# Loading x in halves of 64 partitions on two queues, in a Trainium2 kernel that sums a gated long convolution and a gated MLP

## The chip, the cores and the metric

The kernel runs on one core of a Trainium2 chip. The metric is the device time of one execution in microseconds (us), of which three runs of the kernel before are known: 233.98, 233.99 and 234.03, median 233.99. One execution was also taken by the profiler; its trace covers 232.4 us from the first instruction to the last.

## The reference

```python
x  = A_q                                   # (1, 2048, 640) bf16
xn = layernorm(x)                          # over the 640 features, no gain or bias
# branch A: a short convolution of k over 4 taps, times v, then a convolution over all
# 2048 positions with ssm_k (by FFT of length 4096), a skip term, and a gate by xn
kv = shift_conv(A_k, A_shift_k) * A_v
a  = xn * (irfft(rfft(kv) * rfft(A_ssm_k))[:2048] + kv * A_ssm_D)
# branch B: a gated MLP, 640 -> 1728 -> 640
b  = (sigmoid(xn @ B_w_gate) * (xn @ B_w_up)) @ B_w_down
out = x + a + b
```

## The kernel before, in words

The 2048 rows of x are laid out as 128 partitions by 16 blocks: row 16p + b stands on partition p in block b, so one block is 128 rows of 640 bf16 values, 1280 bytes each and 160 KB together, with its rows 20 KB apart in DRAM. Tile `x` holds all blocks; it receives the results too (`down_ev`, L320, and `inv2_x`, L498, add into it) and is stored to `out` from there (`store`, L323).

The MLP runs in four groups `t` of four blocks (512 rows). Group 0 has to be normalised before any product can start, and this is the opening that the change touches:

1. L501 to L505 load the blocks 0 to 3. Blocks 0 and 1 load as two column halves each, columns 0 to 319 on SP's queue (`sync`) and columns 320 to 639 on ACT's queue (`nc.scalar`). Block 2 is one transfer on SP, block 3 one on ACT. Each queue so issues 80, 80 and 160 KB.
2. L506 to L508 put the first four weight loads (320 KB each) behind them on SP: gate and up columns 0 to 255, then gate and up columns 256 to 511.
3. For each block VectorE (DVE) takes the statistics of the two column halves (`ln_stats`, L198), joins them (L202) and adds epsilon (L210); GpSimd (POOL) takes the power -0.5 (L214); DVE writes the normalised block (`ln_xn`, L219). TensorE (PE) turns it in five transposes (`xn_mm`, L244), and ScalarE (ACT) copies the turned block out of PSUM (`xn_ev`, L247).
4. PE meanwhile runs 10 products on zeros (`busy`, L515), and 3 more after block 0's transposes. Then come the quarter products (`quarter`, L262), a block of 128 rows at a time for the first two feature tiles of gate and up, each needing one turned block. From the third feature tile on, whole products of 512 rows run (`product`, L271).

After that, every step of the kernel comes from a string of letters written out by hand (`ORDER`), each letter the next step of one chain: "g" the MLP's products, "m" the early loads, "o" the stores, and so on. The tail of the order is the last `down_mm` steps, with the last block's columns 512 to 639 as the very last product, then `down_ev` on DVE, then the store of those 128 columns (L662): 128 rows of 256 bytes, 32 KB, on SP.

The compiled program gives each DMA one of eight completion semaphores in turn. A DMA whose semaphore was used before waits, on the engine that issues it, until the earlier DMA with that semaphore has landed. Before, six x loads and the first two weight loads take the eight semaphores, and the third weight load is the first that waits.

Of the kernel before, what the change touches and what calls it, by code (L numbers as in the profile page):

```python
# [17 lines left out]
DM = 640  # L18
FF = 1728
P = 128  # L20
NB = S // P
# [36 lines left out]
def kernel(  # L58
# [14 lines left out]
    nc = tc.nc  # L73
    xr = A_q.flatten_outer_dims().rearrange("(p b) d -> p b d", b=NB)
    kr = A_k.flatten_outer_dims().rearrange("(p b) d -> p b d", b=NB)
    vr = A_v.flatten_outer_dims().rearrange("(p b) d -> p b d", b=NB)
    outr = out.flatten_outer_dims().rearrange("(p b) d -> p b d", b=NB)
# [27 lines left out]
    x = res.tile([P, NB, DM], BF16, name="x")  # L105
# [15 lines left out]
    sync = nc.sync  # L121
# [201 lines left out]
        sync.dma_start(outr[:, b0:b1, lo:hi], x[:, b0:b1, lo:hi])  # L323


    def add_D(c):
        h0 = cin[c]["kvh"][0:1, 1, 0:2, :].rearrange("p b c -> p (b c)").rearrange("p (c e) -> p e c", e=2)[:, 0, :]
        nc.gpsimd.tensor_tensor(h0, h0, cin[c]["dr"][:, :], ALU.add)
# [169 lines left out]
        nc.vector.tensor_tensor(xs, xs, chunks[c]["yx", m][:, :, :], ALU.add)  # L498


    for b in range(2):  # L501
        for i in range(2):
            (sync, nc.scalar)[i].dma_start(x[:, b, 320 * i:320 * i + 320], xr[:, b, 320 * i:320 * i + 320])
    for i in range(2):
        (sync, nc.scalar)[i].dma_start(x[:, 2 + i, :], xr[:, 2 + i, :])  # L505
    for lo in (0, 256):  # L506
        for u in range(2):
            load_w(sync, lo, lo + 256, u)  # L508
# [43 lines left out]
    def step(k, fn, *args):  # L552
        chains[k].append((fn, args))
# [48 lines left out]
    for c in range(NC):  # L602
        for n in range(2):
            step("H", h_turn, c, n)
        step("D", add_D, c)
        for n in range(8):
            step("a", st1_mm, c, n)
# [51 lines left out]
    for b in range(12, NB - 1):  # L659
        step("o", store, b, b + 1, 0, DM)  # L660
    step("o", store, NB - 1, NB, 0, 4 * P)
    step("o", store, NB - 1, NB, 4 * P, DM)  # L662

    ORDER = """
    mmggmmsgmuggmsgmgsuZumgggssumkgkguskugkkmsgugmmmmgkgmksgmuggHskkHkgsmukkgDumsgggkusumgTmkgkukagaumHg
# [44 lines left out]
```

## Time and profile before

| what | value |
|---|---|
| median of three runs | 233.99 us (233.98 to 234.03) |
| profiled execution: span | 232.4 us |
| PE busy | 227.3 us, 98% of the span |
| DVE busy | 203.9 us, 88% |
| ACT busy | 123.0 us, 53% |
| SP's DMA queue (q1) | 90.6% of 16 engines' span |
| ACT's DMA queue (q10) | 0.5% |
| first DMA issue / first statistics on DVE | 0.72 us / 3.02 us |
| last instruction of DVE ends | 229.89 us |

The profile records the span of its execution only; the runs' time is 1.6 us longer than the span. Busy time of PE is modelled for pipelined matmuls, so that neighbouring rows overlap. A DMA row is the issue on the engine that issues it ("SPq", "ACTq"); the transfer itself runs later, and the profile gives for some of them the time from issue to landing. All times in a view are from the span's start.

### The profile page before, as it was taken

How to read it: one execution, taken by the hardware profiler on the slowest of the kernel's cores; microseconds unless marked ns; L12 is line 12 of the kernel's file. 1: busy time of each engine (PE TensorE's matmuls, PEld its weight loads, DVE VectorE, ACT ScalarE, POOL GpSimd, SP SyncE). 2: the span in 40 equal slices, each digit the busy share in tenths (PEclk: the TensorE clock that was granted, in tenths of full speed). 3: DMA queues.
4: the chain of work that ended last, by engine and by line, in shares of the span. 5: the costliest groups of instructions: out<-in, count | busy, mean ns of one | idle time of the engine just before them, and what ended most of it. 6: DMA issues, size and time to landing. Idle time of an engine off the chain costs nothing.

```text
span 232.4 us, 5436 instructions
## 1 busy us (share of the span) xinstructions
PE 227.3 (98%) x2201; PEld 130.7 (56%) x2201; DVE 203.9 (88%) x362; ACT 123.0 (53%) x154; POOL 13.3 (6%) x26
## 2 busy tenths in 40 slices
PE   7999999999999999999999999999999999999995
PEld 2754445877454556667554544478654544446772
DVE  5534799999989999999999999997799999997773
ACT  2433232595354877766775847673555667752000
POOL 5210010040001100000010300000000000000000
PEclk9999999999999999999999999999999999999999
DMA  6999999799999979999989999597989998364784
GB/s 179 320 328 238 265 312 293 201 249 148 336 209 322 290 263 241 273 210 237 331 236 268 272 258 300 171 218 203 260 247 276 290 257 246 119 170 115 224 265 136
DMA packets 96303, 56.79 MB, mean 244 GB/s; under 512 B 55894, under 2 KB 90518, under 8 KB 96022
## 3 DMA queue, kind: packets, MB, share of 16 engines
q1 hardware_dynamic: 95846, 56.12, 90.6%
q8 instruction: 17, 0.28, 0.5%
q10 hardware_dynamic: 432, 0.33, 0.5%
q14 instruction: 8, 0.07, 0.1%
HBM read 36.12 MB, written 18.35 MB: 234 GB/s over the span
## 4 chain that ended last, share of the span: by engine, by line
PE 95%; DVE 2%; DMA 1%; ACT 0%; issue 0%
PE pd L315 27%; PE pu L271 24%; PE pg L271 24%; PE psb L488 4%; PE ps L376 4%; PE ps L374 4%; PE ps L418 3%; PE psa L447 2%; PE pg L292 2%; DVE st L198 1%; DMA x<-in_A_q_dram 1%; PE pu L262 1%; PE pg L262 1%; PE pt L244 0%; DVE xn L219 0%; ACT xnT L247 0%
## 5 line engine op out<-in xcount | busy, mean ns | idle before, releaser
L271 PEld LDWEIGHTS <-w 128*128 128x128 bf16 x500 | 46.6, 98 | 54.2 <-issue 4.7
L315 PE MATMUL pd<-wd,hT 128*128 128x320 bf16 (+2 forms) x448 | 66.0, 299 | 0.0
L271 PE MATMUL pg<-xnT,w 128*128 128x512 bf16 x250 | 62.2, 379 | 0.1
L271 PE MATMUL pu<-xnT,w 128*128 128x512 bf16 x250 | 62.2, 379 | 0.0
L315 PEld LDWEIGHTS <-hT 128*128 128x128 bf16 x448 | 41.7, 98 | 18.2 <-issue 2.4
L280 ACT ACTIVATE sig<-pg 128x512 bf16<-128x512 f32 x52 | 31.1, 601 | 31.1 <-PE pg L271 27.3
L286 DVE TENSOR_TENSOR hT<-sig,pu 128x512 bf16<-128x512 bf16 x52 | 34.9, 680 | 11.6 <-PE pu L271 7.5
L234 ACT CAST xz<-ps 128x1024 bf16<-128x1024 f32 x36 | 35.1, 1014 | 15.8 <-PE ps L418 15.7
L234 ACT CAST t<-ps 128x1024 bf16<-128x1024 f32 x24 | 23.7, 1013 | 16.3 <-PE ps L376 14.1
L433 DVE TENSOR_TENSOR xz<-xz 128x2048 bf16<-128x2048 bf16 x20 | 24.4, 1219 | 0.2
L376 PE MATMUL ps<-kvh,S1t 128*128 128x128 bf16 x160 | 21.4, 219 | 0.0
L374 PE MATMUL ps<-kvh,S1t 128*128 128x128 bf16 x160 | 21.4, 217 | 0.0
L354 DVE TENSOR_TENSOR acc<-acc,tmp 128x1024 bf16<-128x1024 bf16 x30 | 20.4, 681 | 0.3
L352 DVE TENSOR_TENSOR tmp<-kx,sc 128x1024 bf16<-128x1024 bf16 x30 | 20.4, 680 | 0.3
L320 DVE TENSOR_TENSOR x<-pd,x 128x320 bf16<-128x320 f32 (+2 forms) x32 | 15.2, 482 | 3.8 <-PE pd L315 3.6
L374 PEld LDWEIGHTS <-S1t 128*128 128x128 bf16 x160 | 15.5, 97 | 2.5
L376 PEld LDWEIGHTS <-S1t 128*128 128x128 bf16 x160 | 15.4, 96 | 2.5
L234 ACT CAST TBt<-ps 128x1024 bf16<-128x1024 f32 x14 | 13.8, 1012 | 4.0 <-PE ps L376 3.9
L198 DVE BATCH_NORM_STATS2 st<-x 128x6 f32<-128x320 bf16 x32 | 13.9, 475 | 1.9 <-DMA x<-in_A_q_dram 1.9
L493 DVE TENSOR_TENSOR yx<-psb,xn 128x512 bf16<-128x512 f32 x20 | 13.7, 686 | 1.4 <-PE psb L488 0.8
L431 DVE STREAM_SHUFFLE xz<-xz 128x512 f32<-128x512 f32 x20 | 14.6, 728 | 0.0
L234 ACT CAST ao<-psa 128x1024 bf16<-128x1024 f32 x9 | 9.0, 1013 | 8.3 <-PE psa L447 6.9
(55 smaller groups left out, 159.8 us busy)
## 6 DMA issues: line engine op xcount, KB each, us to landing
t<-d SPq DMA_DIRECT2D x15, 512.0 KB, 6.0
d<-t SPq DMA_DIRECT2D x13, 512.0 KB, 4.9
d<-TBt SPq DMA_DIRECT2D x7, 512.0 KB, 5.8
d<-ao SPq DMA_DIRECT2D x6, 512.0 KB, 5.5
bi<-d SPq DMA_DIRECT2D x6, 512.0 KB, 5.3
kx<-in_A_k_dram SPq DMA_DIRECT2D x10, 256.0 KB, 5.9
hn<-in_A_ssm_k_dram SPq DMA_DIRECT2D x20, 128.0 KB, 5.0
kvh<-in_A_v_dram SPq DMA_DIRECT2D x10, 256.0 KB, 5.2
```

What stands on the lines that cost most here:

```text
L198: nc.vector.bn_stats(d["st"][:, i, s2, :], x[:, b, s2 * 320:(s2 + 1) * 320])
L234: nc.scalar.copy(out=out, in_=in_)
L271: nc.tensor.matmul(pg[:, :], lhsT=w[:, c, u * UP + fc * P:u * UP + (fc + 1) * P], rhs=xnT[:, :, c, :], start=(c == 0), stop=(c == NC - 1))
L280: nc.scalar.activation(sig[fc][:, :], pgs[0, fc][:, :], ACT.Sigmoid)
L286: nc.vector.tensor_tensor(hT[:, fc, :], sig[fc][:, :], pgs[1, fc][:, :], ALU.mult)
L315: nc.tensor.matmul(pd[:, :], lhsT=hT[:, fc, bb * P:(bb + 1) * P], rhs=wd[:, fc, es], start=(fc == 0), stop=(fc == NFC - 1))
L320: nc.vector.tensor_tensor(x[:, 4 * t + bb, es], pds[bb, half][:, :], x[:, 4 * t + bb, es], ALU.add)
L352: nc.vector.tensor_tensor(d["tmp"][:, :, :], kx[:, lo + 3 - m:hi + 3 - m, :], sb(m), ALU.mult)
L354: nc.vector.tensor_tensor(d["acc"][:, :, :], d["acc"][:, :, :], d["tmp"][:, :, :], ALU.add)
L374: nc.tensor.matmul(ps[:, i, 0:P], lhsT=S1[:, b, h, :], rhs=cin[c]["kvh"][:, 0, b, :], start=True, stop=True)
L376: nc.tensor.matmul(ps[:, i, P:2 * P], lhsT=S1[:, b, h, :], rhs=hp[:, b // 2, b % 2, :], start=True, stop=True)
L433: nc.vector.tensor_tensor(z[:, 1:3, :, :], z[:, 0:1, :, :].to_broadcast((P, 2, 8, P)), z[:, 1:3, :, :], ALU.mult)
```

## The change

Blocks 0 to 3 load in the same way, each as two transfers of 64 partitions with the full row of 640 values: partitions 0 to 63 on SP, partitions 64 to 127 on ACT. There are eight x loads of 80 KB instead of four of 80 KB and two of 160 KB, four on each queue instead of three. The store of the last 128 columns is split in the same way, 64 partitions on SP and 64 on ACT; the step stays the last one of the chain "o".

```diff
+    def last_store():
+        for i, eng in enumerate((sync, nc.scalar)):
+            eng.dma_start(outr[rows[i], NB - 1, 4 * P:DM], x[rows[i], NB - 1, 4 * P:DM])
+
...
-    for b in range(2):
+    rows = (slice(0, 64), slice(64, P))
+    for b in range(4):
         for i in range(2):
-            (sync, nc.scalar)[i].dma_start(x[:, b, 320 * i:320 * i + 320], xr[:, b, 320 * i:320 * i + 320])
-    for i in range(2):
-        (sync, nc.scalar)[i].dma_start(x[:, 2 + i, :], xr[:, 2 + i, :])
+            (sync, nc.scalar)[i].dma_start(x[rows[i], b, :], xr[rows[i], b, :])
...
-    step("o", store, NB - 1, NB, 4 * P, DM)
+    step("o", last_store)
```

## The prediction

> **What bounds the kernel now.** I read the page's shares first, then who kept PE waiting, then the chain of waits in the first 14 us, then the order of time at both ends.
>
> ```profile
> PE 227.3 (98%) x2201; PEld 130.7 (56%) x2201; DVE 203.9 (88%) x362; ACT 123.0 (53%) x154; POOL 13.3 (6%) x26
> PE 95%; DVE 2%; DMA 1%; ACT 0%; issue 0%
> ```
>
> PE carries 95% of the chain that ended last. The list of PE's waits (us in total, times, longest) has only three entries, all in the opening:
>
> ```profile
> PE idle L515 <- DVE hT L117: 1.2, 1, 1.2
> PE pt L244 <- DVE xn L219: 0.7, 2, 0.4
> PE pg L262 <- ACT xnT L247: 0.2, 1, 0.2
> ```
>
> So once the quarter products run, PE never stops until its last product. The end is the moment at which PE gets going, plus a fixed amount of PE work, plus the tail after the last product. The change touches the first and the last of these. The chain of waits shows what sets the first:
>
> ```profile
> 0.72 2.27 DMA x<-in_A_q_dram
> 2.99 0.02 issue
> 3.02 0.90 DVE st L198 x2
> ...
> 7.04 0.47 PE pt L244 x5
> 7.51 0.02 issue
> 7.53 0.70 ACT xnT L247
> 8.23 0.04 issue
> 8.27 0.72 PE pg L262 x10
> ```
>
> Only one transfer is in it: block 0's, issued at 0.72 and landed at 2.99. Then DVE works without a gap to block 1's normalised rows, PE and ACT turn them, and from 8.27 PE is continuous. Blocks 1 to 3 are not in it: DVE reaches their statistics at 4.25, 5.76 and 7.21, and the semaphore records of the trace have them landed by 3.60, 5.36 and 5.59. A microsecond won or lost at 3.02 is therefore a microsecond of the whole; an earlier landing of block 2 or 3 is worth nothing.
>
> **The opening: the wait that DVE starts on.** Today DVE's first statistics need only the left column half, from SP. The right half, from ACT, landed at 3.18 by the semaphore records, 0.19 later though issued at the same moment, and DVE needs it only after 0.46 us of its own work. With halves by partition, the first statistics span all 128 partitions and wait for both. So the first step of the sum is a loss: with transfers as they are now, DVE starts 0.19 later.
>
> Against this stands a faster transfer. Windows over the opening show what the 16 DMA engines do (last columns: granted clock, DMA share, GB/s):
>
> ```profile
> 1.70:2.20 0.50, 0.50 (x3) 0.17 (x2) 0.00 (x0) 0.50 (x1) 0.50 (x2) 1.00 0.48 122
> 2.20:2.70 0.50, 0.50 (x3) 0.15 (x1) 0.00 (x0) 0.45 (x2) 0.50 (x2) 1.00 1.11 322
> 3.00:3.20 0.20, 0.20 (x2) 0.00 (x1) 0.18 (x1) 0.00 (x0) 0.03 (x1) 1.00 2.27 179
> 3.20:3.70 0.50, 0.50 (x2) 0.15 (x1) 0.50 (x2) 0.00 (x0) 0.00 (x0) 1.00 0.36 65
> ```
>
> Two things in it. First, packet cost: between 2.20 and 2.60 the two queues used 60.5% and 55.5% of 16 engines for 234 packets, 1.16 x 16 x 400 / 234 = 32 ns each, nearly all of 640 bytes. The 1280-byte stores at 228.5 to 230.1 used 86.7% for 430 packets, 46 of them tiny: about 57 ns for one of 1280 bytes. Block 0 is 256 packets of 640 now and 128 of 1280 then: 16 x 32 = 512 ns an engine against 8 x 57 = 456, 0.06 us less. Second, supply: in the first half microsecond of packets the engines are busy 0.48 of the time, because packets arrive one by one. If packets arrive at the same rate but carry twice the bytes, that idle time, 0.5 x 0.52 = 0.26 us, could shrink to nothing; it could also stay, if it comes from how fast each engine's queue is opened. So block 0's second half lands between 3.18 - 0.06 - 0.26 = 2.86 and 3.18. I take the packet term whole and a quarter of the supply term, 3.18 - 0.06 - 0.06 = 3.06, since the later queue opens when the engines are already filling (322 GB/s from 2.20 on). Against 2.99 that is **+0.07 us**, bounds -0.13 and +0.19.
>
> The Trainium skill has a rule that speaks against this edit (page "DMA: Bandwidth & Descriptors", section "Rules for kernel authors"): two transfers to disjoint partition halves serialise, since both spray over all 16 engines, and one transfer of 128 partitions is to be used. The trace agrees that both queues share the engines (60.5% and 55.5% in one window); by the rule the supply term would be nothing, and the opening +0.13.
>
> **What else moves in the opening.** The issues: SP issues four x loads instead of three, at 0.40 to 0.45 us each, so the first gate weights go out at about 2.55 to 2.6 instead of 2.12. This costs nothing: their data waits behind the x data anyway (they landed at 6.63, and PE first wants them at 7.33, 0.70 later). The cover is that 0.70. The semaphores: eight x loads fill the eight, but the first gate load takes one that ACT has not yet reached, so ACT's last x load (block 3, partitions 64 to 127) waits for block 0's landing, and the first up weights wait for block 0 as well. ACT's load goes out at about 3.1 instead of 1.65. Behind it on ACT stands the copy of the turned block 0 at 6.08, 3 us away. The load needs, by ACT's slower issue-to-landing times (2.5 us by the semaphore records for block 0, 3.9 for block 3), until 5.6 to 7.0; DVE wants it at 7.21. Hidden, by 0.2 us in the worst of the two. The up weights go out at 3.1 instead of 2.59; they landed at 7.75 and PE wants them at 9.11, cover 1.36. All later weight loads wait for the DMA eight places before them, as they do now. Orders on PE, DVE and POOL are the same line for line.
>
> **The tail.** DVE's last addition ends at 229.89. SP issues the last store at 229.97; it lands 1.5 us later, at 231.475, and the program's closing waits run to 232.4.
>
> ```profile
> 228.57 1.77 SPq L323 DMA_DIRECT2D out_dram<-x  x3
> 228.82 1.07 DVE L320 TENSOR_TENSOR x<-pd,x 128x512 bf16<-128x512 f32 x2 [1.15 <-PE pd L315]
> out_dram<-x SPq DMA_DIRECT2D x1, 32.0 KB, 1.5
> ```
>
> Its 128 packets of 256 bytes ran from 230.85 to 231.12, right behind the store before it, which itself landed at 231.25. Halving them saves at most 0.22 us (the store before then ends the program). But now the end waits for an ACT issue as well. ACT is free (its last work ends at 211.9), so nothing is queued behind it, but no row shows ACT issuing a store or anything late. The nearest rows are the opening's: ACT's transfer landed 0.19 (block 0) and 0.2 (3.9 against 3.7 us for blocks 3 and 2) later than SP's twin. Its first packet came 1.26 us after the issue, against 0.88 for the last store on SP: 0.38 is the upper bound. I take 0.2, less 0.07 for four packets fewer an engine at 18 ns: **+0.13 us**, bounds -0.22 and +0.38.
>
> **The sum.** +0.07 + 0.13 = +0.20 on a span of 232.4. The runs' median lies 1.6 us above the span; what lies outside the span does not change, so I add to the median: 234.2 us, +0.09%. A measurement of this kernel tells about 0.2%, 0.47 us, from no change, and the sum is inside that. The bounds together are -0.35 and +0.57: 233.6 to 234.6.
>
> **The rivals.**
>
> *Slower: the stall catches block 0.* In the windows above, DMA throughput collapses from 3.00 to 3.70 (179 and 65 GB/s at up to 2.27 times full share: packets in flight for 0.3 to 1 us). These slow packets are the first 1280-byte ones of blocks 2 and 3; no 640-byte packet took over 0.24. If the stall belongs to that size or row pattern and not to the moment, block 0 meets it. Price, by the rate lost against 331 GB/s: 0.2 x 0.46 + 0.5 x 0.80 = 0.49 us, so +0.69 and 234.7. It decides as soon as 0.27 of the 0.49 falls before block 0's landing. Against it: packets of other sizes are slow too, in bursts all over the trace, and 1280-byte stores late are not. Chance 0.20.
>
> *Slower: ACT's queue is late at both ends.* +0.19 and +0.38 together give +0.57, 234.6. For it: every ACT transfer in the trace is later than its SP twin. Against: smaller transfers should not be as late as larger ones. Chance 0.07.
>
> *Faster: the supply term whole and short issues.* If 64 rows are generated in half the time, block 0 lands at 2.86, and a shorter issue (0.26 us for a one-row load against 0.40) takes 0.14 more; with the tail at its floor, -0.13 - 0.14 - 0.22 = -0.49, 233.5. It needs everything at its best end. Chance 0.13.
>
> *Block 3's ACT half late.* If it queues behind the up weights (landed 7.75) DVE waits 0.5 us at 7.21. The fourth normalised block is done at 9.85 and PE takes it at 10.22, so 0.37 is covered: +0.13 more, 234.3, still no change. Chance 0.05. That the halves are not what runs is excluded by the program: 64x640 loads on both queues.
>
> **How the numbers follow.** The forecast holds 0.55. Within 0.2%: forecast and late block 3, 0.60. Slower: 0.20 + 0.07 = 0.27. Faster 0.13. The range reaches from the edge of the faster case, 233.55, to a little over the stall's price, 234.8; about 0.08 is left out below and as much above. The forecast alone would be 233.7 to 234.45.
>
> **What would show it.** After: DVE's first statistics start at 3.05 to 3.15 with both halves of block 0 landed by then; the statistics stay gapless; PE's quarter products run on from about 8.35; the ACT store lands after the SP one, at about 231.7. A start of DVE before 2.9 says that the supply term was whole; one after 3.4 that a stall came in. A PE wait later than 8.5, or one on weights, would make the reasoning wrong, not only its sizes.

## The result, and the profile after

The changed kernel takes 235.91 us (median of six runs, 235.32 to 237.35). The kernel before took 234.07 (six runs, 233.98 to 234.36). The ratio is 1.0083, 95% interval 1.0056 to 1.0111: slower by 0.8%, and outside the predicted range of 233.55 to 234.8. Two things happened: even the fastest run is 1.34 us above the fastest of before, and the runs of the changed kernel spread over 2 us.

The profiled execution took 235.32, the fastest of the six; its span is 233.5, against 232.4 before. The page:

```profile
PE 227.9 (98%) x2201; PEld 130.9 (56%) x2201; DVE 204.1 (87%) x362; ACT 123.1 (53%) x154; POOL 13.3 (6%) x26
PE 75%; SPq 11%; DVE 6%; DMA 6%; issue 1%; DVEq 0%
```

PE's work is unchanged, but the chain that ended last no longer runs through PE alone: 11% of it is SP issuing DMAs, which had no share before, and 6% is DMA (1% before). The list of PE's waits has a fourth entry, in the middle of the kernel:

```profile
PE idle L518 <- DVE hT L117: 1.2, 1, 1.2
PE pt L244 <- DVE xn L219: 0.7, 2, 0.4
PE pg L262 <- ACT xnT L247: 0.2, 1, 0.2
PE ps L378 <- DVE kvh L361: 0.2, 1, 0.2
```

The opening in order of time (start, duration, engine, line):

```profile
0.72 0.56 ACTq L508 DMA_DIRECT2D x<-in_A_q_dram  x1
0.72 2.77 SPq L508 DMA_DIRECT2D x<-in_A_q_dram  x4
1.37 1.19 ACTq L508 DMA_DIRECT2D x<-in_A_q_dram  x2
3.10 0.47 ACTq L508 DMA_DIRECT2D x<-in_A_q_dram  x1
3.46 0.49 DVE L198 BATCH_NORM_STATS2 st<-x 128x6 f32<-128x320 bf16 x1 [2.34 <-DMA x<-in_A_q_dram]
3.54 0.59 SPq L173 DMA_DIRECT2D w<-in_B_w_gate_dram  x1
```

Each x issue keeps its queue for 0.47 to 0.81 us, where those of before took 0.40 to 0.45. Four of them occupy SP for 2.77 us, so the first weight load goes out at 3.54 instead of 2.12, 1.42 later. DVE starts at 3.46 instead of 3.02, 0.44 later. By the semaphore records ACT's half of block 0 landed first, at 3.08, and SP's at 3.36; the half that DVE needed first before had landed at 2.99. So 0.37 of the 0.44 is the landing. The other 0.07 is a second wait: in all the kernels that were profiled, DVE starts 0.10 after the landing where it waits for two loads, and 0.02 to 0.03 after it where it waits for one. The windows that the prediction used now read:

```profile
1.70:2.20 0.50, 0.50 (x3) 0.18 (x2) 0.00 (x0) 0.50 (x1) 0.50 (x2) 1.00 0.19 28
2.20:2.70 0.50, 0.50 (x3) 0.15 (x1) 0.00 (x0) 0.49 (x2) 0.50 (x2) 1.00 0.86 264
3.00:3.20 0.20, 0.20 (x2) 0.01 (x1) 0.00 (x0) 0.00 (x0) 0.03 (x1) 1.00 1.01 199
3.20:3.70 0.50, 0.50 (x2) 0.15 (x1) 0.24 (x1) 0.00 (x0) 0.00 (x0) 1.00 1.02 264
```

From 1.70 to 2.20 the engines move 28 GB/s, not 122, because the first packet comes at 2.07 instead of 1.76 (ACT's; SP's first comes at 2.44). The supply of packets did not get better but worse. The collapse at 3.2 to 3.7 (65 GB/s before) is gone, so the stall that the prediction feared is not the cause.

The tail:

```profile
229.41 1.07 DVE L320 TENSOR_TENSOR x<-pd,x 128x512 bf16<-128x512 f32 x2 [1.15 <-PE pd L315]
230.52 0.53 ACTq L328 DMA_DIRECT2D out_dram<-x  x1
230.56 0.54 SPq L328 DMA_DIRECT2D out_dram<-x  x1
```

The two stores leave at the moment that one would, but each issue takes 0.53 or 0.54 instead of 0.375. By the semaphore records ACT's half lands at 232.27 and SP's, issued 0.05 after it, at 232.55. From DVE's last end (230.49) to the last landing are 2.07 us; it was 1.58.

The profiled span so divides: PE gets going 0.46 later (whole products from 13.21 instead of 12.75); PE and DVE lose 0.13 on the way to the last addition; the last landing comes 0.49 later after it; the closing instructions take 0.10 more. Together 1.18.

### The profile page after: what moved, and what is told of

It is laid out like the page before. It is cut to its first block, busy times and chain, and to the rows that moved or that the text cites. A ratio compares the mean times of both kernels' runs of the same rounds, so it can differ in the third digit from the quotient of the medians.

```text
span 233.5 us, 5444 instructions
## 1 busy us (share of the span) xinstructions
PE 227.9 (98%) x2201; PEld 130.9 (56%) x2201; DVE 204.1 (87%) x362; ACT 123.1 (53%) x154; POOL 13.3 (6%) x26
## 4 chain that ended last, share of the span: by engine, by line
PE 75%; SPq 11%; DVE 6%; DMA 6%; issue 1%; DVEq 0%
PE pd L315 21%; PE pu L271 18%; PE pg L271 18%; PE psb L492 4%; PE ps L378 3%; PE ps L380 3%; PE ps L422 3%; DMA x<-in_A_q_dram 3%; DMA kvh<-in_A_v_dram 3%; PE psa L451 2%; SPq L173 2%; SPq L176 2%; SPq L139 2%; PE pg L292 1%; DVE st L198 1%
```

## The experiments

The first theory was read off the rows above: **an issue of 64 partitions is dear in itself**, and it costs in three places, DVE's start, SP's stream of loads behind it, and the tail. The rivals: that it is dear only when both queues issue halves together, that it comes from splitting and waiting for two queues, or that only DVE's start and the tail count.

### What an issue costs, by itself

The loop of the first measuring kernel, without the definitions above it (the comment is added here):

```python
for f in 2 * (sp_full, sp_lo, sp_hi, sp_cols, sp_lo_cols, sp_32, sp_96, sp_64x2, act_full, act_lo,
              pair_cols, pair_rows, pair_full):
    nc.vector.memset(y[:, 0:2, :], 0.0)   # holds the next load until this one has landed
    f()
```

> This kernel computes nothing of the reference: it issues single loads of x rows by themselves, each after the one before has landed and DVE has cleared the tile, twice over: on SP 128, 64 (partitions 0 to 63), 64 (64 to 127), 32 and 96 partitions of 640 values, 128 and 64 partitions of 320, 64 partitions of two rows of 320; on ACT 128 and 64 of 640; then pairs on both queues. Theory 'an issue of 64 partitions is dear in itself': every load of 64 partitions keeps its queue 0.15 to 0.25 us longer (about 0.6 us) than one of 128 partitions (about 0.4), alone as well as in pairs, whatever its bytes. Rival 'only together': alone 64 and 128 partitions both take 0.35 to 0.45, and 0.6 only in the pair of partition halves. Rival 'packet size': 64 of 640 takes 0.6, 64 of 320 and 64 of two rows take 0.4.

The kernel ran once. Rows of its timeline, in this order: SP's loads of 64 partitions (0 to 63), 64 (64 to 127), 128 x 320, 64 x 320, 32, 96, two rows of 320 on 64 partitions, and, in the second pass, 128:

```profile
11.26 0.53 SPq L92 DMA_DIRECT2D y<-in_A_q_dram  x1
14.52 0.47 SPq L92 DMA_DIRECT2D y<-in_A_q_dram  x1
17.55 0.33 SPq L92 DMA_DIRECT2D y<-in_A_q_dram  x1
20.34 0.47 SPq L92 DMA_DIRECT2D y<-in_A_q_dram  x1
23.20 0.35 SPq L92 DMA_DIRECT2D y<-in_A_q_dram  x1
25.87 0.32 SPq L92 DMA_DIRECT2D y<-in_A_q_dram  x1
28.71 0.64 SPq L101 DMA_DIRECT2D y<-in_A_q_dram  x1
48.75 0.33 SPq L92 DMA_DIRECT2D y<-in_A_q_dram  x1
```

All the forms with 64 partitions take 0.47 or more, alone on an otherwise idle core; all the others on SP take 0.32 to 0.35, those of 32 and 96 partitions too. So both rivals fail: a load of 64 is dear alone, and with 640 bytes per packet as with 1280 (two rows per partition make it dearer still, 0.64). The difference, 0.14, is a little under the 0.15 to 0.25 that was expected; in the kernel, where one issue follows another, both forms take longer, about 0.42 and 0.60. The packet records add what the issue rows hide: the first packet starts 0.97 us after the issue for 128 partitions and 1.27 for 64, so 0.30 is lost before any data moves. A whole 128-partition block landed after 2.14 us and a 64-partition half, with half the bytes, after 2.15 to 2.38.

The pairs show how block 0 loads in the two kernels. Column halves: SP's landed 2.09 and 2.17 us after the issue (two passes), ACT's 2.27 and 2.34. Partition halves: 2.34 and 2.44, and 2.60 and 2.68. DVE needs SP's column half in the one kernel, the later of both partition halves in the other: 2.09 against 2.60, 0.51 later. The kernel shows 0.44. In the pair ACT's first packet comes 0.17 and 0.19 after SP's for columns, and 0.26 and 0.32 after it for partition halves. This second delay is not special to 64 partitions: with a whole block on each queue it is 0.32 and 0.30. Nor is it always ACT that is later: in the changed kernel SP's first packet came 0.37 after ACT's.

### Which row counts, and the store

The second measuring kernel has the same loop over other forms.

> Like the first measuring kernel (nothing of the reference is computed): single loads of 640 values on SP with 128, 16, 48, 56, 63, 64 (from partition 32), 65, 72, 80 and 112 rows; of two rows of 320 on 32, 96 and 128 partitions; then 96 rows on SP with 32 on ACT; then stores of 128 columns to DRAM: 128 partitions on SP, on ACT, 64 on SP, 64 + 64, 96 + 32, and 64 + 64 columns. 'Exactly 64 rows is dear': only the load from partition 32 takes about 0.47, the others 0.33; 'a range of row counts': some of 48 to 80 take 0.47 too. Stores: 64 on SP takes 0.15 longer to issue than 128; the pair of 64 + 64 lands 0.3 to 0.5 later than the whole store on SP, the pair 96 + 32 within 0.2 of it.

It ran once, too. Loads of 63, 64 (from partition 32), 65 and 72 rows, then the store of 128 partitions on SP and that of 64:

```profile
19.70 0.27 SPq L92 DMA_DIRECT2D y<-in_A_q_dram  x1
22.46 0.61 SPq L92 DMA_DIRECT2D y<-in_A_q_dram  x1
25.62 0.31 SPq L92 DMA_DIRECT2D y<-in_A_q_dram  x1
28.39 0.30 SPq L92 DMA_DIRECT2D y<-in_A_q_dram  x1
52.24 0.37 SPq L97 DMA_DIRECT2D out_dram<-y  x1
56.96 0.51 SPq L97 DMA_DIRECT2D out_dram<-y  x1
```

Of the counts that were tried (16, 48, 56, 63, 64, 65, 72, 80, 112, 128, and 32 and 96 in the first kernel) 64 alone is dear. Landing times of the stores, from the semaphore records, two passes each: whole on SP 1.48 and 1.45 us after the issue, whole on ACT 1.49 and 1.51, 64 partitions on SP alone 1.75 and 1.71, the later one of 64 + 64 1.97 and 1.96, of 96 + 32 1.59 and 1.62, of column halves 1.64 and 1.58. So 64 + 64 costs 0.49 to 0.51 over the whole store, which is the 0.49 of the kernel's tail, and no split of this store wins anything. About half of it is the form alone (1.71 to 1.75 against 1.45 to 1.48), the other half the second place in a pair. The pair of loads of 96 and 32 rows landed 2.30 and 2.28 us after the issue on SP, 2.47 and 2.43 on ACT, also later than SP's column half (2.09 and 2.17). Why 64 is special no run shows.

### The opening alone, the tail alone

The changed kernel with the last store of before:

```diff
-    step("o", last_store)
+    step("o", store, NB - 1, NB, 4 * P, DM)
```

> The opening of the changed kernel with the last store of the kernel before. If the two places add up as in the profiles (PE starts 0.46 us later, about 0.1 us of a wait in the middle, tail 0.5), this one is 0.5 to 0.9 us slower than before in its best runs, with the same spread upwards of 1 to 2 us, since the spread comes from loads that the opening delays; if the spread came from the tail, this one is steady within 0.3 us.

Measured: 235.58 median, lowest 234.56, highest 237.26, where before's 25 runs on that chip had 234.29, 233.86 and 235.86. Ratio 1.0041, interval 1.0010 to 1.0073. Lowest run +0.70, median +1.29, and the spread is there without the split store.

The changed kernel with the opening of before:

```diff
-    for b in range(4):
+    for b in range(2):
         for i in range(2):
-            (sync, nc.scalar)[i].dma_start(x[rows[i], b, :], xr[rows[i], b, :])
+            (sync, nc.scalar)[i].dma_start(x[:, b, 320 * i:320 * i + 320], xr[:, b, 320 * i:320 * i + 320])
+    for i in range(2):
+        (sync, nc.scalar)[i].dma_start(x[:, 2 + i, :], xr[:, 2 + i, :])
```

> The opening of the kernel before with the last store split over both queues. Theory 'longer issue and a late second landing': the end moves by 0.4 to 0.6 us after DVE's last addition, the time by as much (234.4 to 234.7), steady from run to run. By the forecast's own tail term it would be +0.13 (234.2).

Measured: 234.76, lowest 234.41: +0.47 and +0.55; ratio 1.0025, interval 1.0000 to 1.0050. In its profile the last landing is 2.08 us after DVE's last end. The size is as expected; "steady" is a miss, since its runs reach 236.25. But those of before reach 235.86 on the same chip, so the split store need not be the reason. The two halves of the change add up about: 0.70 + 0.55 = 1.25 in the lowest runs against 1.34, and 1.29 + 0.47 = 1.76 in the medians against 1.84.

### SP's stream late, DVE's start not

Against the kernel before:

```diff
+    nc.gpsimd.memset(w[:, 0, 0:1], 0.0)
+    nc.gpsimd.memset(w[:, 0, UP:UP + 1], 0.0)
     for lo in (0, 256):
         for u in range(2):
             load_w(sync, lo, lo + 256, u)
```

> The kernel before, with x loaded as before, but the first weight loads on SP held back until GpSimd has cleared one column of the weight tile (about 3.2 us instead of 2.12): SP's stream is late by about 1.1 us and DVE's start is not. Theory 'the late stream costs by itself': waits appear in the middle (DVE for x's second group of blocks, PE behind it) and the time is 0.3 to 1.5 us longer with a spread. Rival 'only DVE's start and the tail count': the time stays within 0.2 us of before.

Measured: 235.69, lowest 234.62: +1.40 and +0.76; ratio 1.0058, interval 1.0031 to 1.0085. Its profile is of the slowest of its ten runs, 237.27. In it DVE starts at 2.95, and the first weight load goes out at 3.11. The waits of PE and, from 9 to 60 us, of DVE:

```profile
PE ps L374 <- DVE kvh L357: 1.4, 1, 1.4
...
PE ps L374 <- DMA S1t<-tabS: 0.9, 1, 0.9
...
PE ps L374 <- ACT t L234: 0.5, 1, 0.5
```

```profile
DVE kvh L334 <- DMA hn<-in_A_ssm_k_dram: 2.4, 2, 2.1
DVE acc L348 <- DMA kx<-in_A_k_dram: 1.6, 1, 1.6
...
DVE st L198 <- DMA x<-in_A_q_dram: 0.5, 1, 0.5
```

Nothing at PE's start (whole products from 12.79), nothing in the tail (1.58 us): a microsecond on SP's stream comes out again between 22 and 58 us, as waits on later loads of SP, most of them for the convolution. The rival "only DVE's start and the tail count" is refuted by the lowest run as well as by the median; the size of these waits is that of the slowest run. The changed kernel's own profile has the same waits, small, since it is the fastest run:

```profile
DVE st L198 <- DMA x<-in_A_q_dram: 0.3, 1, 0.3
DVE acc L352 <- DMA kx<-in_A_k_dram: 0.2, 1, 0.2
```

### The same split at 96 and 32

Against the changed kernel, at both places:

```diff
-    rows = (slice(0, 64), slice(64, P))
+    rows = (slice(0, 96), slice(96, P))
```

> The changed kernel with 96 and 32 partitions instead of 64 and 64, at both places: same number of transfers, queues, semaphores and waits. 'The dear issue of 64 rows is the cause': DVE starts at 3.0 to 3.15, SP's first weight load goes out at about 2.6, the tail is within 0.2 us of before; time 234.2 to 234.6, the blind forecast's world. Rival 'splitting by partition and waiting for both queues costs, whatever the row count': as the changed kernel, 235.3 to 237.

Measured: 234.62, lowest 234.37, against 234.20 and 233.98 for before: +0.42 and +0.39; ratio 1.0022, interval 1.0006 to 1.0038. The opening:

```profile
0.72 1.81 SPq L508 DMA_DIRECT2D x<-in_A_q_dram  x4
2.57 0.43 SPq L173 DMA_DIRECT2D w<-in_B_w_gate_dram  x1
3.27 0.89 DVE L198 BATCH_NORM_STATS2 st<-x 128x6 f32<-128x320 bf16 x2 [2.16 <-DMA x<-in_A_q_dram]
```

Number of transfers, queues, semaphores and waits are those of the changed kernel. With issues of 0.40 to 0.43 on SP the first weights leave at 2.57, not 3.54, and the tail takes 1.68 us instead of 2.07. So the dear form of 64 rows makes most of the change: 1.34 in the lowest runs shrinks to 0.39. What is left is the cost of the split as such, by this profile 0.25 at DVE's start (3.27 against 3.02) and 0.10 in the tail. The start was expected at 3.0 to 3.15 and is later: SP's 96 rows landed at 3.17, and the second wait adds its 0.07. This profile is of the slowest of its twelve runs (236.07). It shows a wait in the middle: 1.5 us of PE behind DVE's L361, itself behind `hn` and x loads.

### Two versions with fewer issues on SP

The kernel before with whole blocks (only the new lines are shown):

```diff
+    for b in range(4):
+        (sync, nc.scalar)[b % 2].dma_start(x[:, b, :], xr[:, b, :])
```

> The kernel before with blocks 0 to 3 as whole 128-partition transfers, 0 and 2 on SP, 1 and 3 on ACT. From the first measuring kernel (two whole blocks on both queues landed 2.7 to 2.9 after issue) DVE starts at 3.4 to 3.6, as late as in the changed kernel; but SP has two x issues of 0.33 to 0.42 and sends its weights at about 1.7. 'DVE's start counts one for one': 0.4 to 0.6 slower in its best runs. 'The late stream makes the spread': less spread than before, and a median that is closer to its lowest than the changed kernel's.

Measured: 235.20, lowest 234.84 (+1.00, +0.86); ratio 1.0045, interval 1.0029 to 1.0061. Two expectations are missed: the lowest run was expected at +0.4 to +0.6, and median minus lowest is 0.36, not less than the 0.22 of before on the same chip. The profile, of the slowest of the twelve runs (236.37), shows two losses in the opening, while SP's stream is early (first weights at 1.66):

```profile
4.12 0.89 DVE L198 BATCH_NORM_STATS2 st<-x 128x6 f32<-128x320 bf16 x2 [3.00 <-DMA x<-in_A_q_dram]
PEclk9799999999999999999999999999999999999999
```

DVE started at 4.12, later than 3.4 to 3.6: block 0 landed 3.37 us after its issue, some of its packets were in flight for 0.3 to 0.8 us, and from 2.20 to 2.70 the engines moved 156 GB/s instead of 322. So the whole blocks met a stall of the kind that the prediction feared. And PE's granted clock was 0.50 from 8.2 to 11.6 us (the 7 in the second slice of the page's row), while every other kernel's profile has 1.00 until its products are done. PE's whole products began at 15.09, 2.34 later than before: 1.10 from DVE's start and 1.24 from the clock. Why the clock fell no run shows. So this experiment tells little about the theory of the late stream.

The kernel before with halves of 64 partitions for blocks 0 and 1 alone (`rows` as in the changed kernel):

```diff
     for b in range(2):
         for i in range(2):
-            (sync, nc.scalar)[i].dma_start(x[:, b, 320 * i:320 * i + 320], xr[:, b, 320 * i:320 * i + 320])
+            (sync, nc.scalar)[i].dma_start(x[rows[i], b, :], xr[rows[i], b, :])
```

> The opening with halves of 64 partitions for blocks 0 and 1 alone; blocks 2 and 3 whole as before, and the last store as before. DVE's start must be as late as in the changed kernel (3.4 to 3.5), since block 0 loads in the same way, but SP has two issues of 0.6 and one of 0.42, so that its first weight load goes out at about 2.5 to 2.6 instead of 3.54. 'Two costs, DVE's start and the late stream': lowest run 0.4 to 0.5 above before, with the spread of before (median minus lowest 0.2 to 0.4), so a median of 234.5 to 234.9 against 235.6 for the whole opening. Rival 'the spread comes from DVE's late start': median as the whole opening, 235.3 to 235.9.

Measured: 234.80, lowest 234.43 (+0.51, +0.47); ratio 1.0024, interval 0.9997 to 1.0052. DVE starts at 3.52, as late as in the changed kernel; the first weights leave at 2.88 (later than expected: the whole block's issue behind the dear ones took 0.60 too). The opening alone had +0.70 in the lowest run and +1.29 in the median, each against before on its own chip. So with DVE's start as late and the first weights 0.66 earlier, both are smaller, the median much more, as was forecast. It is not a clean separation of the two costs. The late weights alone cost 0.76 in the lowest run too, and the profile here (234.75, near the median) has a loss of its own, a wait for block 1:

```profile
5.13 0.49 DVE L198 BATCH_NORM_STATS2 st<-x 128x6 f32<-128x320 bf16 x1 [0.29 <-DMA x<-in_A_q_dram]
```

PE's whole products start at 13.57, 0.36 later than in the changed kernel, and PE waits for nothing after the opening. What is shown is that DVE's late start and SP's late stream each cost time; how much of the spread belongs to which is not shown.

### A try for something better

Against the kernel before:

```diff
-    for i in range(2):
-        (sync, nc.scalar)[i].dma_start(x[:, 2 + i, :], xr[:, 2 + i, :])
+    for b in (2, 3):
+        nc.scalar.dma_start(x[:, b, :], xr[:, b, :])
```

> A version meant to beat both: the opening of before, but block 2 loads on ACT too, so that SP has two x issues and sends its weights 0.45 us earlier (about 1.65). 'The stream on SP makes the spread': lowest run as before, the upper half of the runs closer to it, median 0.1 to 0.3 below that of before. Rival 'blocks 2 and 3 now come too late': block 3 waits for block 0's semaphore and shares the DMA engines with the weights; if it lands after 7.2, DVE waits and it is 0.1 to 0.6 slower.

Measured: 235.47, lowest 235.07 (+1.18, +1.11); ratio 1.0046, interval 1.0029 to 1.0063. The rival holds. ACT's last load waits for block 0's semaphore, goes out at 3.16 behind three weight loads, and lands at 8.82. In the profile, of the slowest of its eight runs, DVE meets it:

```profile
3.36 0.89 DVE L198 BATCH_NORM_STATS2 st<-x 128x6 f32<-128x320 bf16 x2 [2.24 <-DMA x<-in_A_q_dram]
...
8.84 0.89 DVE L198 BATCH_NORM_STATS2 st<-x 128x6 f32<-128x320 bf16 x2 [1.21 <-DMA x<-in_A_q_dram]
```

DVE's first start, at 3.36, is late as well, though block 0 loads as before. Here ACT's packets came first (1.75, SP's at 2.00; before, SP's at 1.76 and ACT's at 1.98), and SP's half landed at 3.34 instead of 2.99. So which queue's packets come first differs between profiles, and here DVE's start was a third of a microsecond later with it.

No version that was run beats the kernel before.

## Why the prediction was wrong, point by point

**The bound.** That the end is PE's start plus fixed work plus the tail was nearly right for the profiled run, the fastest: the two ends make 0.46 and 0.49 of its 1.18 (forecast: 0.07 and 0.13), and the middle 0.13. It was incomplete: it took PE's list of waits as proof that nothing in between was near the limit. The trace of before shows that SP's loads had little to spare. The load of k that DVE waits for at L348 landed at 22.14 and was used from 22.25, a cover of 0.11; x's second group landed at 42.80 and was used from 43.34, a cover of 0.54. By the prediction's own sign, a PE wait later than 8.5 us (0.2 us, ending at 55.3), its reasoning was wrong here and not only its sizes. Before's own runs reach 236.38 on one of the chips; whether from these loads is not shown, as only its fastest run was profiled. The profile of the split store alone (234.79), which has before's opening, shows another source: block 2 landed at 6.00 instead of 5.36, and PE's whole products began 0.27 later.

**The supply term: the step that failed first.** The prediction wrote "if packets arrive at the same rate but carry twice the bytes", took -0.06 from it and bounded it at nothing. The first packet of a 64-partition transfer comes 0.30 later, and the first packet of the pair's second transfer another 0.26 to 0.37 after that. The later half of block 0 was forecast to land between 2.86 and 3.18 and landed at 3.36. With the 0.07 of the second wait, which the prediction did not have, DVE's start moved by +0.44, outside the bounds of -0.13 and +0.19. The sign that a start after 3.4 means a stall misled: the start was at 3.46 and there was no stall. The Trainium skill advises against two transfers to disjoint partition halves (page "DMA: Bandwidth & Descriptors", section "Rules for kernel authors"), and the runs agree with the advice: the later half of a pair landed after 2.60 to 2.68 us, one whole transfer after 2.14. The +0.13 that the prediction worked out from it was under a third of the cost.

**The issues: a term put at nothing.** "SP issues four x loads instead of three, at 0.40 to 0.45 us each" priced a 64-row issue as one of 128 rows. It takes 0.60 to 0.81 on SP here. The four cost SP 1.42 us more, where about 0.46 was forecast. "This costs nothing" held for the first weights, whose cover of 0.70 was checked, and failed for what is queued behind them on SP: the loads of k, ssm_k, v and x's second group, wanted by DVE from 22 us on, which nobody had checked. The late stream alone, by 0.99 us, cost 0.76 in the lowest run and 1.40 in the median. The trace of before held a warning: `wd`'s last load (L184), with 64 rows of 640, took 0.79 us to issue at 28.98. It gives no price by itself, as the issues beside it took 0.58 to 1.73.

**The tail.** +0.13 with a bound of +0.38; it was +0.49. The direction was right, the place was not: ACT's half was to land last, and SP's did. The missing part is again the form of 64 partitions: alone it lands 0.25 to 0.28 later than the whole store, and the second of a pair lands another 0.22 to 0.26 later.

**The rivals.** The stall did not occur in the changed kernel; the whole blocks met one. "ACT's queue late at both ends" was near in form (both ends, +0.57), but its cause is the row count and not ACT: alone, ACT's whole store lands like SP's (1.49 against 1.48), and in the changed kernel ACT's half was the earlier one at both ends. Block 3's late half was hidden as forecast in the changed kernel (landed 6.03, wanted at 7.67); the last experiment shows that a late block 3 has a price (DVE waited 1.21).

## What to carry to other kernels

Before a transfer is cut into pieces, take the issue time of that very shape from a row of the trace or measure it alone: the shape can cost more than the bytes save, and what counts is first packet and landing, not issue alone. When an in-order queue gets a longer prologue, check the cover of everything behind it up to the first place where the queue drains, not only of the next transfer. A wait list that is empty in one trace does not say how much slack there is; the times between landing and first use do, and so does delaying one stream on purpose.

## What the runs showed of the hardware that was not expected

A DMA of exactly 64 partitions takes 0.47 to 0.61 us to issue, alone or with two rows per partition (0.63 to 0.64), as load or store, on SP or ACT, from partition 0, 32 or 64; one of 63 or 65 takes 0.27 and 0.31, one of 128 takes 0.33. Its first packet comes 0.28 to 0.30 later. Of two DMAs issued on SP and ACT at the same moment, one sends its first packet later than the other: by 0.17 and 0.19 us for loads of 128 partitions with 320 values, 0.30 and 0.32 with 640, 0.48 and 0.52 for 96 + 32 partitions, 0.26 to 0.37 for 64 + 64, and only 0.06 to 0.09 for stores of 96 + 32 partitions or of column halves. Which of the two is first differs between profiles. DVE starts 0.10 us after the last landing where it waits for two loads, 0.02 to 0.03 where it waits for one. In one run PE's granted clock was 0.50 for 3.4 us of the opening, at a cost of 1.24 us. Why 64 is dear stays open.
